# Attention, channel mix and mixer on one core: a pair's first two tiles of queries share one step for scores, one bias and one step for products

## The chip, the cores and the metric

The kernel runs on one core of a Trainium2 chip. Its engines are TensorE (PE, with PEld for the loading of weights), VectorE (DVE), ScalarE (ACT), GpSimd (POOL) and SyncE (SP), which issues the DMAs. Each engine works through its own instructions in order. The metric is the device time of one execution in microseconds, median of several runs.

## The reference

Three layers follow each other, all in fp32, for 4 batches of 576 tokens: attention with 8 heads of 64 and a mask by blocks of 64 tokens, a channel mix with a shift by one token, and a mixer over tokens and channels.

```python
def _attn_ref(q, k, v):                      # (4, 8, 576, 64) each
    scores = scale * np.matmul(q, k.transpose(0, 1, 3, 2))
    mask = block_i >= block_j                # blocks of 64 tokens
    scores = np.where(mask, scores, -1000000000.0)
    scores = scores - np.max(scores, axis=-1, keepdims=True)
    attn = np.exp(scores)
    attn = attn / (np.sum(attn, axis=-1, keepdims=True) + 1e-09)
    return np.matmul(attn, v).astype(np.float32)

def _moe_ref(x, mu_k, mu_r, w_k, w_v, w_r):  # x (4, 576, 512)
    xk = mu_k * x + (1.0 - mu_k) * x_prev    # x_prev: x one token earlier
    xr = mu_r * x + (1.0 - mu_r) * x_prev
    k = np.maximum(xk @ w_k, 0.0)
    v = k * k @ w_v
    r = 1.0 / (1.0 + np.exp(-(xr @ w_r)))
    return (r * v).astype(np.float32)

def _moe2_ref(x, w_tok1, w_tok2, w_ch1, w_ch2):
    h = np.maximum(x.transpose(0, 2, 1) @ w_tok1, 0.0) @ w_tok2
    u = x + h.transpose(0, 2, 1)
    h2 = np.maximum(u @ w_ch1, 0.0) @ w_ch2
    return (u + h2).astype(np.float32)
```

## The kernel before

**Layout.** The 8 heads are taken as 4 pairs. The 576 tokens of a batch are two parts: part 0 is tokens 0 to 255, with the query tiles j = 0 and 1 of 128 rows, part 1 is tokens 256 to 575, with j = 2, 3 and a last one, j = 4, of 64 rows for both heads together. `attention(b, hf)` issues, for each pair, the loads of q and k (`load_qk`) and of v (`load_v`, with v scaled to fp16 halves vb), one `unit` for each query tile, and `pv`.

**unit.** A tile's scores (L510) go into a PSUM tile s of two banks, one for each head; two such tiles are there. DVE masks the block above the diagonal (L538) and takes the negated maximum of the rows (L544), the bias is that times 0.125 (L553 on DVE; L551 on ACT for j = 1, by `nb_a`), ACT takes the exponentials with their sums (L563), and the reciprocal of the sum (L575 or L571, then L581) scales them. The probabilities become two fp16 tiles side by side in `pin`, a rounded one (`first`: L587 on ACT where j stands in `p1_act` or, in the batch's opening, `p1_first`, else DVE) and what the rounding left (`second`, L593 on DVE). A DMA from SP transposes pin into pt (`turn`, L599). `pv.products` multiplies pt with vb into the PSUM tile o (L646), `pv.total` scales o into xt (L655 on ACT for part 1, L657 on DVE for part 0).

**Channel mix.** For each part, `mix` builds the operands in fp32 pieces: mt (L720 ACT, L726 DVE), its high part xh (L732, on DVE for two of the four) and its low part xl (L736). `r_group` multiplies them with w_r (L751 for xh, L756 for xl) into a PSUM tile l, of which there are two, and `r_out` (L792, ACT) reads it; k_group, k_out and v_group follow in the same manner with w_k and w_v. The mixer's two stages, `front` and `back`, come behind all batches' attention; `back` fills the end of the span (L764).

**Weights.** `load_split` brings each weight in chunks through a DMA (L345), a cast on ACT (L352), a join on DVE (L355), a high part on ACT (L361) and a low part on POOL or DVE (L364). w_r and w_k come in chunks of 410 columns through a stage wst, w_v in 16 chunks of 256 columns through qkl and tw. These run beside the attention of batch 0.

**Order.** Nothing runs in the order in which it is written. Each piece of work is a `step` with an engine, an estimated cost, what it reads and writes, and a key. `Plan.schedule` plays all steps through a model and takes, on each engine, the ready step with the smallest key. The key is the step's due time less the numbers in PLAN: `lead_of` for its kind of step, `lead_begin` on top for the groups in `begin` (the weights of the first layers and batch 0), and `shift` for its group (a010 is attention of batch 0, part 1, pair 0; c00 the channel mix of batch 0, part 0).

Of the kernel before, what the change touches and what calls it, by code (L numbers as in the profile page):

```python
# [46 lines left out]
    nb_a=(1,), sm_a=(1,), ot_a=(1,), nq=(0, 1), sq_1=(), fifo=("xh", "xl", "l", "o", "xt0", "xt1", "qkh", "uh"),  # L47
    ft=3.02, fd=27.4576, cw=3.3876, tfr=24.8747, lx=0.15, lpe=0.2, lse=0.12, land=2.1,

    lead_of={  # L50
        "attention.edge": -710.03, "back.<lambda>": 34.98, "back.g_group": -21.39, "back.g_high": -674.45,
        "back.g_low": -16.35, "back.rest": 162.8, "back.split": -271.85, "back.store": -779.77, "back.y_group":
        -49.32, "back.y_out": 128.07, "channel_mix.k_group": 0.52, "channel_mix.k_high": 122.36, "channel_mix.k_low":
        49.5, "channel_mix.k_out": 700.87, "channel_mix.r_group": -1.88, "channel_mix.r_out": 38.93,
        "channel_mix.square": -490.37, "channel_mix.store": 972.64, "channel_mix.v_group": -4.31, "channel_mix.v_out":
        138.59, "front.back_in": 734.14, "front.h1_high": -268.59, "front.h1_low": -80.29, "front.hidden": 281.6,
        "front.high": 274.43, "front.load": 776.08, "front.low": 678.84, "front.sum_u": 443.53, "front.turn": -120.46,
        "load_qk.high": 253.03, "load_qk.load": 185.56, "load_qk.low": 404.0, "load_qk.whole": 421.84,
        "load_v.gather": -15.3, "load_v.largest": -10.87, "load_v.load": 459.86, "load_v.one": 31.7, "load_v.power":
        182.97, "load_v.scale": 265.33, "load_v.spread": 478.19, "load_v.two": 729.5, "mix.here": -3.03, "mix.high":  # L60
        -14.49, "mix.low": 3.37, "mix.shifted": 147.07, "pv.products": -2.92, "pv.total": 92.69, "split_chunk.high":
# [56 lines left out]
def c_v2(n):  # L118
    return 0.067 + n / 1920
# [186 lines left out]
class Kern:  # L306
# [1063 lines left out]
```

## Time and profile before

| | |
|---|---|
| time, median of 3 runs | 806.55 us (803.76 to 809.64) |
| profiled execution, its own time | 811.06 us |
| its span, first to last instruction | 809.3 us |
| mean granted clock of TensorE | 0.993 |
| busy: PE, DVE, ACT, POOL | 763.7, 477.3, 419.2, 181.3 us |
| matmuls | 6120 |

The profile is of one execution. The span lies 1.8 us under that execution's time, and the execution 4.5 us over the median. Times in views are microseconds from the start of the span unless marked ns; L12 is line 12 of the kernel. A group or row names output and inputs as out<-in; the granted clock is a share of full speed.

### The profile page before, as it was taken

What the parts mean: (1) busy time and instruction counts of PE and PEld (TensorE: products, weight loads), DVE (VectorE), ACT (ScalarE), POOL (GpSimd) and SP (SyncE); (2) the same over time, 40 slices, a digit from 0 to 9 for tenths busy, and PEclk for the clock granted to TensorE, in tenths of its full rate; (3) what the DMA queues carried; (4) which work ended last, traced back from release to release, by engine and by line L of the source; (5) the groups of instructions that cost most, each with busy time, mean ns of one, the idle gap of its engine ahead of it and who ended that gap; (6) DMA issues with size and microseconds to landing.
All of it is one profiled execution on the core that took longest, in us unless ns stands there. A gap on an engine that the chain in (4) does not pass through costs nothing.

```text
span 809.3 us, 16129 instructions
## 1 busy us (share of the span) xinstructions
PE 763.7 (94%) x6120; PEld 661.7 (82%) x6120; DVE 477.3 (59%) x1194; ACT 419.2 (52%) x1070; POOL 181.3 (22%) x209
## 2 busy tenths in 40 slices
PE   2459999998999999999999999999999999999998
PEld 1227899887989999999999989998888888888886
DVE  7897898997798987789555687612212302301210
ACT  6887978687678795778564565502201201301100
POOL 3433524334145142432443222200000000000000
PEclk9999999999899999999999999999999999999999
DMA  8976964686465843566552654200000010000001
GB/s 272 269 189 106 201 148 115 146 170 120 113 138 125 159 117 93 117 140 113 191 180 84 232 170 141 78 27 1 14 26 1 14 39 14 1 26 14 14 13 40
DMA packets 136750, 84.30 MB, mean 104 GB/s; under 512 B 110944, under 2 KB 118240, under 8 KB 136160
## 3 DMA queue, kind: packets, MB, share of 16 engines
q1 hardware_dynamic: 136672, 83.27, 41.8%
q8 instruction: 48, 0.79, 0.4%
q14 instruction: 30, 0.25, 0.1%
HBM read 47.58 MB, written 9.44 MB: 70 GB/s over the span
## 4 chain that ended last, share of the span: by engine, by line
PE 81%; DVE 7%; DMA 5%; ACT 5%; issue 2%; SPq 0%; POOL 0%; ACTq 0%; DVEq 0%
PE b L764 37%; PE l L751 18%; PE l L756 9%; PE s L510 5%; PE o L646 4%; PE b L938 3%; PE b L959 3%; DMA pt<-pin 3%; DVE pin L593 2%; DMA wst<-in_w_k 1%; PE b L914 1%; DVE nm L544 1%; ACT pin L587 1%; ACT p L563 1%; DMA qkl<-in_w_v 1%
## 5 line engine op out<-in xcount | busy, mean ns | idle before, releaser
L1030 ACT ACTIVATE wy<-b 128x512 fp32r<-128x512 f32 (+1 forms) x60 | 33.3, 555 | 211.8 <-PE b L764 211.2
L764 PE MATMUL b<-uh,wx 128*128 128x512 f32 (+1 forms) x480 | 139.6, 373 | 0.0
L751 PE MATMUL l<-xh,wx 128*128 128x256 f32 (+1 forms) x768 | 123.7, 302 | 2.2 <-ACT r L792 1.8
L751 PEld LDWEIGHTS l<-xh,wx 128*128 128x128 f32 x768 | 107.9, 190 | 7.4 <-ACT r L792 2.0
L764 PE MATMUL b<-wy,c2a 128*128 128x512 f32 (+1 forms) x460 | 110.8, 367 | 0.0
L764 PEld LDWEIGHTS b<-uh,wx 128*128 128x128 f32 x480 | 87.2, 188 | 17.3 <-issue 0.2
L764 PEld LDWEIGHTS b<-wy,c2a 128*128 128x128 f32 x460 | 79.2, 189 | 15.3
L593 DVE SCALAR_TENSOR_TENSOR pin<-p,rs,pin 128x128 f16<-128x128 f32 (+4 forms) x112 | 77.0, 707 | 7.5 <-ACT pin L587 7.3
L1045 DVE TENSOR_TENSOR x<-b,x 128x256 f32<-128x256 f32 (+7 forms) x32 | 13.5, 454 | 114.8 <-PE b L764 114.8
L751 PE MATMUL l<-kh,wy 128*128 128x256 f32 (+1 forms) x512 | 78.1, 304 | 0.2 <-DVE ve L428 0.2
L646 PEld LDWEIGHTS <-vb 128*64 128x64 f16 x1920 | 52.9, 115 | 29.8 <-issue 13.7
L646 PE MATMUL o<-pt,vb 128*64 128x128 f16 (+1 forms) x1920 | 62.4, 220 | 14.3 <-DMA pt<-pin 7.2
L764 PE MATMUL b<-gx,wx 128*128 128x512 f32 x192 | 75.4, 393 | 0.0
L751 PEld LDWEIGHTS l<-kh,wy 128*128 128x128 f32 x512 | 71.5, 194 | 2.5 <-issue 1.4
L563 ACT ACTIVATE p<-s,nb 128x384 f32<-128x384 f32 (+4 forms) x112 | 61.6, 553 | 19.2 <-DVE nb L553 9.7
L587 ACT ACTIVATE pin<-p,rs 128x128 f16<-128x128 f32 (+4 forms) x112 | 63.2, 588 | 13.2 <-DMA pt<-pin 6.9
L756 PE MATMUL l<-xl,wx 128*128 128x320 f32 (+1 forms) x384 | 68.2, 300 | 0.0
L544 DVE TENSOR_REDUCE nm<-s 128x2 f32<-128x256 f32 (+4 forms) x80 | 63.6, 798 | 1.9 <-PE s L510 1.3
L756 PEld LDWEIGHTS l<-xl,wx 128*128 128x128 f32 x384 | 56.6, 190 | 2.1 <-issue 1.2
L1033 DVE SCALAR_TENSOR_TENSOR wy<-b,wy 128x512 fp32r<-128x512 f32 (+1 forms) x28 | 16.1, 576 | 62.8 <-ACT wy L1030 62.7
L1033 DVE SCALAR_TENSOR_TENSOR gx<-b,wy 128x512 fp32r<-128x512 f32 x32 | 21.9, 690 | 47.8 <-ACT wy L1030 47.8
L736 POOL TENSOR_TENSOR xl<-mt,xh 128x256 fp32r<-128x256 f32 (+1 forms) x32 | 28.4, 891 | 91.7 <-DVE xh L732 52.5
(116 smaller groups left out, 1397.0 us busy)
## 6 DMA issues: line engine op xcount, KB each, us to landing
wst<-in_w_c SPq DMA_DIRECT2D x24, 256.0 KB, 2.7
qkf<-in_kq SPq DMA_DIRECT2D x12, 480.0 KB, 3.5
v<-in_v SPq DMA_DIRECT2D x16, 320.0 KB, 3.1
x<-xd SPq DMA_DIRECT2D x4, 1152.0 KB, 7.0
wst<-in_w_c2a SPq DMA_DIRECT2D x18, 256.0 KB, 2.7
qkl<-in_w_v SPq DMA_DIRECT2D x16, 256.0 KB, 3.4
wst<-in_w_k SPq DMA_DIRECT2D x9, 410.0 KB, 5.4
qkf<-in_kq SPq DMA_DIRECT2D x12, 256.0 KB, 2.9
```

The source lines that it names most:

```text
L510: self.nc.tensor.matmul(o, q[e, q0:q0 + P], k[e, k0:k1], start=n == 0, stop=n == len(terms) - 1)
L544: nc.vector.tensor_reduce(out=c["nm"][:, :nh], in_=m, axis=AX.XY if j == 4 else AX.X, op=ALU.max, negate=True)
L563: nc.scalar.activation(out=c[x], in_=s, func=AF.Exp, scale=0.125, bias=c["nb"][:, x:x + 1], accum_out=c["sm"][:, x:x + 1],)
L587: nc.scalar.activation(out=like(pin[:, :n]), in_=c[x], func=AF.Copy, scale=rs)
L593: nc.vector.scalar_tensor_tensor(out=like(pin[:, w:w + n]), in0=c[x], scalar=rs, in1=like(pin[:, :n]), op0=ALU.mult, op1=ALU.subtract)
L646: nc.tensor.matmul(o[hh * D:hh * D + D, q0:q0 + rows], v[:, i, y, hh, :], st["pt", hh, j][:, x * (j + 1) + i, :], start=i == x == y == 0, ...
L736: (nc.vector if i in pl["xl_d"] else nc.gpsimd).tensor_tensor(out=l, in0=x[i], in1=raw(x["h"][i]), op=ALU.subtract)
L751: self.nc.tensor.matmul(ps, ww[:, k, :], x[0][k], start=k == 0 and n == 0, stop=False)
L756: self.nc.tensor.matmul(ps, w[0][:, k, :], x[1][k], start=False, stop=k == kt - 1)
L764: self.nc.tensor.matmul(ps, ww[k], xx[k], start=k == 0 and n == 0, stop=k == kt - 1 and n == 2)
L1030: nc.scalar.activation(out=gh(m), in_=d["g", m][:, :n], func=AF.Relu)
L1033: nc.vector.scalar_tensor_tensor(out=gl(m), in0=d["g", m][:, :n], scalar=0.0, in1=raw(gh(m)), op0=ALU.max, op1=ALU.subtract)
```

## The change

`unit` takes a tuple of tiles. In part 0 a pair's tiles j = 0 and 1 are one unit: their scores are one step into one s tile, the second tile's columns behind the first's in each head's bank, and one bias instruction of 4 columns serves both (on DVE, as the unit's first tile, 0, isn't in `nb_a`). Maximum, exponentials, sums, roundings and transposes stay one for each tile and head. The products of tiles 0 and 1 are one step; those of 2, 3 and 4 stay single. Tile 2 leaves `p1_act`, so its `first` goes from ACT to DVE in batches 1 to 3 (24 instructions). `ft`, which sets when the mixer's first stage is due, goes from 3.02 to 2.94, and all of `lead_of`, `lead_begin` and `shift` have new numbers, so the whole program is ordered anew. The matmuls stay 6120, and the other totals of instructions stay but for the 16 biases and the 24 firsts.

```diff
-    wk=-29.6677, wv=-2.34, cpk=1.6637, cpv=2.1596, p1_act=(0, 1, 2, 3, 4), p1_first=(0, 1, 2, 3, 4), xl_d=(0, 2),
+    wk=-29.6677, wv=-2.34, cpk=1.6637, cpv=2.1596, p1_act=(0, 1, 3, 4), p1_first=(0, 1, 2, 3, 4), xl_d=(0, 2),
...
+    nb_a=(1,), sm_a=(1,), ot_a=(1,), nq=(0, 1), pj=((2,), (3,), (4,)), sq_1=(), fifo=("xh", "xl", "l", "o", "xt0",
+    "xt1", "qkh", "uh"), ft=2.94, fd=27.4576, cw=3.3876, tfr=24.8747, lx=0.15, lpe=0.2, lse=0.12, land=2.1,
...
-    def unit(self, key, st, heads, j, begin):
+    def unit(self, key, st, heads, js, begin):
...
+        nh = 1 if js == (4,) else 2
+        size = lambda j: P * (j + 1) if j < 4 else S
+
+        at, o = {}, 0
+        for j in js:
+            at[j] = o
+            o += size(j)
+        m = nh * len(js)
         c = {}
...
+        each = [(i, j, x) for i, j in enumerate(js) for x in range(nh)]
+        tp, tpin, tpt = ({(j, x): Buf(t or f"pt{j}") for _, j, x in each} for t in ("p", "pin", ""))
...
         def scores():
+            for j in js:
+                n, q0 = size(j), P * j - (j > 1) * NK0
+                if j < 4:
+                    self.qk(st, q0, [(s[:, y, at[j]:at[j] + n], half[y], 0, n) for y in range(2)])
+                else:
+                    self.qk(st, q0, [(s[:, y, :HT], slice(0, P), y * HT, (y + 1) * HT) for y in range(2)])
...
+        def bias():
+            c["nb"] = small("nb")
+            if first_j in pl["nb_a"]:
+                nc.scalar.mul(c["nb"][:, :m], c["nm"][:, :m], 0.125)
             else:
+                nc.vector.tensor_scalar(out=c["nb"][:, :m], in0=c["nm"][:, :m], scalar1=0.125, scalar2=None, op0=ALU.mult)
...
+        def first(i, j, x):
+            pin = c["pin", j, x] = self.pin[tpin[j, x].slot]
+            rs, out = c["rs"][:, row(i, x)], like(j, pin[:, :size(j)])
+            if act(j):
             else:
+                nc.vector.tensor_scalar(out=out, in0=c[j, x], scalar1=rs, scalar2=None, op0=ALU.mult)
...
+        step("PE", cost, key, scores, r=st["tqk"], w=[ts], mode="half" if nh == 2 else "")
+        for i, j in enumerate(js):
+            if j < 4:
+                step("V", 0.14, key, mask, j, w=[(ts, ("mask", j))])
+            n = size(j)
+            step("V", c_v(n if j == 4 else 2 * n), key, largest, i, j, r=[(ts, ("mask", j))], w=[(tnm, i)])
+        step(*(("A", 0.1) if first_j in pl["nb_a"] else ("V", 0.067)), key, bias, r=[tnm], w=[tnb], alone=nh == 1)
+        for i, j, x in each:
+            step("A", c_a(size(j), True, True) + 0.09, key + 0.3 * x, exps, i, j, x,
+                 r=[tnb] if here(j) else [ts, tnb], w=[(ts, (j, x)) if here(j) else tp[j, x], (tsm, (j, x))])
+        for i, j in enumerate(js):
+            r, w = [(tsm, (j, x)) for x in range(nh)], [(trs, j)]
+            step(*(("A", 0.1) if j in pl["sm_a"] else ("V", 0.067)), key, sums, i, j, r=r, w=w, alone=nh == 1)
+            step("V", 0.075, key, inverse, i, r=w, w=w)
+        for i, j, x in each:
+            n, k = size(j), key + 0.3 * x
+            p = (ts, (j, x)) if here(j) else tp[j, x]
+            pin = tpin[j, x]
+            on = ("A", c_a(n, here(j), True)) if act(j) else ("V", c_v(n, True) if here(j) else c_v2(n) + 0.06)
+            step(*on, k, first, i, j, x, r=[p, (trs, j)], w=[(pin, 0)], alone=here(j))
+            step("V", c_v(n, True), k, second, i, j, x, r=[p, (trs, j), (pin, 0)], w=[(pin, 1)], alone=here(j))
+            step("S", 1.24, k, turn, i, j, x, r=[pin], w=[tpt[j, x]], dma=0.224 * (j + 1))
...
-        def products(j):
+        def products(js):
+            for j in js:
+                products_of(j)
+
+        def products_of(j):
...
-        for j in PARTS[hf][2]:
-            step("PE", (0.06 if j < 4 else 0.04) * 4 * (j + 1) + 0.05, key, products, j,
-                 r=[st["tpt", 0, j], st["tpt", 1, j], vst["tvb"]], w=[(to, j)], mode="float16")
+        for js in ((0, 1),) if hf == 0 else PLAN["pj"]:
+            step("PE", sum((0.06 if j < 4 else 0.04) * 4 * (j + 1) for j in js) + 0.05, key, products, js,
+                 r=[st["tpt", x, j] for j in js for x in range(2)] + [vst["tvb"]], w=[(to, js)], mode="float16")
...
-                u = [0.0, 0.33]
-                for j in range(2):
-                    self.unit(t + dt * u[j], st, [0, 1], j, begin)
+                self.unit(t, st, [0, 1], (0, 1), begin)
             else:
                 u = [0.0, 0.32, 0.75]
                 for j in range(2, 5):
-                    self.unit(t + dt * u[j - 2], st, [0, 1], j, begin)
+                    self.unit(t + dt * u[j - 2], st, [0, 1], (j,), begin)
```

In the new kernel's line numbers, exponentials are L573, first L600 (ACT) and L602 (DVE), second L606, the bias on DVE L562, the mix L744, L750, L756 and L760, r_out L816.

The start of ACT's program; wst is the stage of w_r, p, sm and nb the exponentials, their sums and the bias of the first pair. Before:

```order
L563 ACT_TABLE_LOAD
L563 ACTIVATE p,sm<-s,nb 128x128
L352 CAST wst<-wst 128x410
L551 ACTIVATE nb<-nm 128x2
L563 ACTIVATE p,sm<-s,nb 128x128
L563 ACTIVATE p,sm<-s,nb 128x256
L361 CAST wx<-wst 128x410
L587 ACTIVATE pin_90<-p,rs 128x128
```

The table load stood with the exponentials of the first tile, and the bias of the second tile between them. The same engine and place, after:

```order
L352 ACT_TABLE_LOAD
L352 CAST wst<-wst 128x410
L573 ACTIVATE p,sm<-s,nb 128x128
L573 ACTIVATE p,sm<-s,nb 128x256
L361 CAST wx<-wst 128x410
L352 CAST wst<-wst 128x410
L573 ACTIVATE p,sm<-s,nb 128x128
L352 CAST wst<-wst 128x410 x2
```

The table load now stands with the cast of w_r's first chunk, which has moved ahead of all exponentials; those of tile 0 and tile 1 follow each other without a bias between.

ACT around the first r_out (r<-l) of batch 0, part 0; qkl and tw are a chunk of w_v, mt and xh the operands of the mix, xt the output of attention. Before:

```order
L732 CAST xh<-mt 128x256
L720 ACTIVATE mt<-xt_133,omu 128x256
L352 CAST tw_64<-qkl 128x256
L361 CAST wy<-qkl 128x256
L655 ACTIVATE xt_593<-o,vo 128x320
L720 ACTIVATE mt<-xt_131,omu 128x256
L792 ACTIVATE r<-l 128x256
L563 ACTIVATE p,sm<-s,nb 128x384
L361 CAST wy<-qkl 128x256
L732 CAST xh<-mt 128x256
```

The first r_out stands four rows behind a cast of w_v (L352). The same place on ACT, after:

```order
L352 CAST tw_63<-qkl 128x256
L744 ACTIVATE mt<-xt_137,omu 128x256
L361 CAST wy<-qkl 128x256
L744 ACTIVATE mt<-xt_133,omu 128x256
L573 ACTIVATE p,sm<-s,nb 128x384
L756 CAST xh<-mt 128x256
L816 ACTIVATE r<-l 128x256
L352 CAST tw_64<-qkl 128x256
L756 CAST xh<-mt 128x256
L681 ACTIVATE xt_569<-o,vo 128x320
L361 CAST wy<-qkl 128x256
```

It now stands six rows behind one such cast and just ahead of the next, and part 1's total (xt, L655 before, L681 after) has moved from ahead of it to behind it.

DVE in batch 1, at a first tile 2 of part 1 (p and pin of 384 columns, after) and at the same stretch of rows before; kh and kl are operands of the channel mix. Before:

```order
L593 SCALAR_TENSOR_TENSOR pin_90<-p,rs,pin_90 128x128
L538 MEMSET s 64x2x64
L544 TENSOR_REDUCE nm<-s 128x2
L593 SCALAR_TENSOR_TENSOR pin_91<-p,rs,pin_91 128x128
L593 SCALAR_TENSOR_TENSOR pin_93<-s,rs,pin_93 128x256
L553 TENSOR_SCALAR nb<-nm 128x2
L845 CAST kh<-kt 128x320
L848 TENSOR_TENSOR kl<-kt,kh 128x320
L593 SCALAR_TENSOR_TENSOR pin_92<-s,rs,pin_92 128x256
```

Here each second (L593) has its first on ACT. DVE in the same stretch of its program, after:

```order
L562 TENSOR_SCALAR nb<-nm 128x4
L562 TENSOR_SCALAR nb<-nm 128x2
L750 SCALAR_TENSOR_TENSOR mt<-xt_1116,mu,mt 128x256
L602 TENSOR_SCALAR pin_90<-p,rs 128x384
L756 CAST xh<-mt 128x256
L606 SCALAR_TENSOR_TENSOR pin_90<-p,rs,pin_90 128x384
L602 TENSOR_SCALAR pin_91<-p,rs 128x384
L587 TENSOR_SCALAR rs<-sm 128x2
L594 RECIPROCAL rs<-rs 128x2
L606 SCALAR_TENSOR_TENSOR pin_91<-p,rs,pin_91 128x384
```

Two firsts (L602, 128x384) have come into DVE's row, each ahead of its second (L606), and the bias of a pair's two tiles is one instruction of four columns.

## Rows read from the trace of the kernel before

**Rows 1.** Page, parts 1 and 4: busy us, share and instructions; the last chain's shares

```profile
PE 763.7 (94%) x6120; PEld 661.7 (82%) x6120; DVE 477.3 (59%) x1194; ACT 419.2 (52%) x1070; POOL 181.3 (22%) x209
...
PE 81%; DVE 7%; DMA 5%; ACT 5%; issue 2%; SPq 0%; POOL 0%; ACTq 0%; DVEq 0%
```

**Rows 2.** Windows: length, busy us of each engine, granted clock, DMA share, GB/s

```profile
0.00:62.00 62.00, 27.86 (x160) 13.69 (x162) 53.51 (x150) 48.11 (x130) 25.77 (x34) 1.00 0.88 243
...
69.90:74.00 4.10, 4.10 (x20) 3.90 (x20) 3.32 (x10) 4.10 (x14) 1.47 (x2) 0.58 0.44 132
74.00:197.00 123.00, 122.21 (x1421) 109.16 (x1420) 108.02 (x296) 102.63 (x274) 46.41 (x51) 1.00 0.68 143
197.00:208.00 11.00, 7.95 (x88) 7.34 (x88) 5.65 (x16) 5.64 (x18) 3.88 (x5) 0.69 0.93 165
208.00:400.00 192.00, 189.89 (x2209) 175.57 (x2208) 161.26 (x422) 146.71 (x383) 65.30 (x69) 1.00 0.56 124
400.00:511.00 111.00, 111.00 (x733) 102.65 (x732) 75.31 (x167) 62.67 (x150) 33.66 (x43) 1.00 0.52 169
```

**Rows 3.** Timeline of PE: start, us, what [idle before, releaser]

```profile
69.90 1.56 PE L751 MATMUL l<-xh,wx 128*128 128x256 f32 x8 [1.76 <-ACT r L792]
...
201.91 1.86 PE L646 MATMUL o<-pt,vb 128*64 128x128 f16 x31 [2.82 <-DMA pt<-pin]
```

**Rows 4.** Timelines of ACT, SP and DVE around 62 to 70 us

```profile
68.00 0.48 ACT L352 CAST tw<-qkl 128x256 f16<-128x256 bf16 x1 [3.62 <-DMA qkl<-in_w_v]
69.48 0.37 ACT L792 ACTIVATE r<-l 128x256 f32<-128x256 f32 x1
...
62.01 0.86 SPq L345 DMA_DIRECT2D qkl<-in_w_v  x1
...
63.93 0.27 DVE L732 CAST xh<-mt 128x256 fp32r<-128x256 f32 x1
```

**Rows 5.** Chain of waits in order of time: start, us, what

```profile
69.90 1.56 PE l L751 x8
...
78.69 0.95 PE l L751 x8
...
86.91 1.01 PE o L646 x32
...
112.99 1.92 PE l L751 x16
...
203.77 3.60 PE l L751 x16
```

**Rows 6.** ACT's first instructions; tile wst: DMAs, durations, time to landing

```profile
6.55 1.28 ACT L563 ACT_TABLE_LOAD   x1 [6.55 <-DVE nb L553]
7.85 0.37 ACT L563 ACTIVATE p<-s,nb 128x128 f32<-128x128 f32 x1
8.21 0.64 ACT L352 CAST wst<-wst 128x410 f16<-128x410 bf16 x1
...
L345 SPq DMA_DIRECT2D wst<-in_w_r x4: 432/432/432, 2.6 to 4.0; - x4
...
DMA to landing us min/median/max: 5.5/6.3/7.2
```

**Rows 7.** Groups by line and form: xcount | busy us, mean ns | idle before, releaser

```profile
L593 DVE SCALAR_TENSOR_TENSOR pin<-p,rs,pin 128x384 f16<-128x384 f32 x32 | 21.6, 690 | 1.8 <-ACT pin L587 1.6
...
L587 ACT ACTIVATE pin<-p,rs 128x384 f16<-128x384 f32 x32 | 19.0, 612 | 2.3 <-DMA pt<-pin 1.8 <-DVE xt L681 0.4
...
L446 DVE SCALAR_TENSOR_TENSOR vb<-v,vs,vb 128x640 f16<-128x640 f32 x16 | 18.2, 1138 | 1.8 <-ACT vb L443 1.7
...
L544 DVE TENSOR_REDUCE nm<-s 128x2 f32<-128x768 f32 x16 | 15.1, 946 | 0.1
...
L593 DVE SCALAR_TENSOR_TENSOR pin<-s,rs,pin 128x256 f16<-128x256 f32 x24 | 11.0, 479 | 6.4 <-ACT pin L587 6.1
...
L544 DVE TENSOR_REDUCE nm<-s 128x2 f32<-128x512 f32 x16 | 10.8, 678 | 0.1
...
L355 DVE SCALAR_TENSOR_TENSOR qkl<-qkl,tw 128x256 uint32<-128x256 uint32 x16 | 8.1, 505 | 2.7 <-ACT tw L352 2.7
...
L732 DVE CAST xh<-mt 128x320 fp32r<-128x320 f32 x16 | 5.3, 337 | 0.0
...
L551 ACT ACTIVATE nb<-nm 128x2 f32<-128x2 f32 x16 | 3.2, 201 | 1.1 <-DVE nm L544 0.9
```

More of the change, by code (lines that the diff above doesn't have):

```diff
@@ L48 @@
-    ft=3.02, fd=27.4576, cw=3.3876, tfr=24.8747, lx=0.15, lpe=0.2, lse=0.12, land=2.1,
+    nb_a=(1,), sm_a=(1,), ot_a=(1,), nq=(0, 1), pj=((2,), (3,), (4,)), sq_1=(), fifo=("xh", "xl", "l", "o", "xt0",
+    "xt1", "qkh", "uh"), ft=2.94, fd=27.4576, cw=3.3876, tfr=24.8747, lx=0.15, lpe=0.2, lse=0.12, land=2.1,
     lead_of={
[L51 to L61, printed above, removed]
-        -63.89, "split_chunk.join": 6.76, "split_chunk.load": 143.85, "split_chunk.low": 282.21, "split_chunk.top":
-        -112.45, "unit.bias": 105.96, "unit.exps": -239.76, "unit.first": -135.83, "unit.inverse": 471.77,
-        "unit.largest": 1.71, "unit.mask": -0.69, "unit.scores": 481.59, "unit.second": 298.83, "unit.sums": 7.56,
-        "unit.turn": -61.72,
@@ new lines @@
+        185.59, "front.back_in": 1124.06, "front.h1_high": -95.34, "front.h1_low": -7.08, "front.hidden": 575.4,
+        "front.high": 539.5, "front.load": 951.26, "front.low": 879.84, "front.sum_u": 705.05, "front.turn": -293.4,
+        "load_qk.high": 205.12, "load_qk.load": 584.15, "load_qk.low": 147.07, "load_qk.whole": 506.8,
+        "load_v.gather": -17.03, "load_v.largest": -21.68, "load_v.load": 418.12, "load_v.one": 230.69,
+        "load_v.power": 513.99, "load_v.scale": 250.78, "load_v.spread": 450.42, "load_v.two": 681.14, "mix.here":
@@ new lines @@
+        -4.95, "mix.high": 30.93, "mix.low": 17.72, "mix.shifted": 349.13, "pv.products": 11.11, "pv.total": 128.96,
+        "split_chunk.high": -127.18, "split_chunk.join": 12.93, "split_chunk.load": 510.1, "split_chunk.low": 672.28,
+        "split_chunk.top": -253.27, "unit.bias": 235.66, "unit.exps": -360.91, "unit.first": -227.18, "unit.inverse":
+        277.04, "unit.largest": -13.48, "unit.mask": 47.55, "unit.scores": 841.0, "unit.second": 253.51, "unit.sums":
+        112.87, "unit.turn": 392.45,
@@ L91 @@
-        19.35, "mix.low": 63.96, "mix.shifted": 223.54, "pv.products": -1.86, "pv.total": 4.3, "split_chunk.high":
-        191.37, "split_chunk.join": -2.04, "split_chunk.load": -58.89, "split_chunk.low": -104.87, "split_chunk.top":
-        225.28, "unit.bias": 146.72, "unit.exps": 56.02, "unit.first": 220.91, "unit.inverse": -61.06, "unit.largest":
-        0.1, "unit.mask": 86.57, "unit.scores": 187.42, "unit.second": -42.99, "unit.sums": -11.55, "unit.turn":
-        -135.86,
+        "attention.edge": 193.5, "back.<lambda>": 170.91, "back.g_group": 188.34, "back.g_high": -146.25,
@@ new lines @@
+        "front.high": 482.71, "front.load": -138.31, "front.low": -393.74, "front.sum_u": 336.72, "front.turn": 55.86,
+        "load_qk.high": -498.1, "load_qk.load": -466.89, "load_qk.low": 760.96, "load_qk.whole": 7.71,
+        "load_v.gather": 317.87, "load_v.largest": -38.89, "load_v.load": -52.74, "load_v.one": 414.52,
+        "load_v.power": 31.61, "load_v.scale": 52.73, "load_v.spread": -277.94, "load_v.two": -477.87, "mix.here":
+        -8.16, "mix.high": 98.86, "mix.low": 144.06, "mix.shifted": 68.56, "pv.products": 100.12, "pv.total": -28.59,
@@ L96 @@
+        "split_chunk.high": 314.93, "split_chunk.join": 159.29, "split_chunk.load": -39.85, "split_chunk.low":
+        -187.23, "split_chunk.top": 211.97, "unit.bias": 74.62, "unit.exps": -178.98, "unit.first": 254.2,
+        "unit.inverse": 89.37, "unit.largest": 40.19, "unit.mask": 30.33, "unit.scores": 49.76, "unit.second": -38.72,
+        "unit.sums": 8.33, "unit.turn": -463.54,
     },
```

135 lines of the change are left out of this document (55 added, 80 removed), and 16 rows, old and new, of the table shift.

## The prediction

> **What bounds the kernel now.** The page's busy shares come first: TensorE (PE) is busy for 94% of the span, VectorE (DVE) for 59%, ScalarE (ACT) for 52%, and the chain that ended last is 81% PE [rows 1]. So PE's work is the floor, and this change leaves PE's work alone: the same 6120 matmuls, in another order. What it can win or lose is idle time of PE and time at half clock. The table of windows says where these lie [rows 2]. In the first 62 us PE has 27.86 us of work, so 34 us pass without it; DVE is busy for 53.51 of them and the DMA engines for 0.88 of their time. From 74 to 197 us PE works 122.21 of 123, from 208 to 400 us 189.89 of 192, from 400 to 511 us 111.00 of 111, and the tail behind 511 us is the last mixer alone, which the change doesn't order anew in any way that shows. Two short places remain. At 69.90 PE had waited 1.76 us for ScalarE's r [rows 3], and in the 4.10 us behind that the granted clock is 0.58 [rows 2]. At 201.91 it had waited 2.82 us for a transposed probability tile [rows 3], and the window around it has 7.95 us of PE in 11 at a clock of 0.69 [rows 2].
>
> The price of each is read from the chain [rows 5]. Eight matmuls of 256 columns take 0.95 us on their normal step and 1.56 at 69.90; sixteen of 320 take 1.92 and, at 203.77, 3.60. [...] First place: 1.76 + 4.10 x (1 - 0.58) = 3.5 us. Second place: 11 - 7.95 = 3.05 idle, 3.60 - 1.92 = 1.7 on the sixteen, and about 0.85 on the 31 products that took 1.86 [rows 3] against 32 in 1.01 [rows 5]: 5.6 us.
>
> **The change part by part.** The sum is made against the profiled execution, 811.06 us (span 809.3); the median shown is 806.55, that is 4.5 lower, and the difference is carried over unchanged.
>
> Merged steps, 0. The scores and the products of a pair's first two tiles have the same matmuls as before, and in the order before, the products of both tiles already stand without a gap in 12 of 16 pairs. Over the whole kernel PE changes kind of work 213 times where it was 218. Nothing there is worth a microsecond. That the first tile's exponentials now wait for the second tile's scores and maximum costs one 128x512 maximum, 0.678 us [rows 7], of lead; from 65 us on PE waits 0.79 us in 123 [rows 2], so the lead hides it. If that cover went, 16 x 0.678 = 10.8 us is the far end, which I don't take.
>
> One bias, 0. Sixteen biases of 0.201 us leave ACT [rows 7], and DVE's stays, with four columns in place of two. ACT is busy for 102.63 of 123 us in the long stretch [rows 2] and doesn't gate it.
>
> The opening, +0.8. Three rows speak. (a) ACT's first instruction was the table load for the exponentials, at 6.55, with the first exponential at 7.85 [rows 6]. In the new order a cast of w_r comes first (first order fence). Its DMA is issued at 2.60 and takes 5.5 us at least [rows 6], so it lands at 8.1, and if the table load stands behind the same wait ACT starts 1.55 us late; if not, the cast's 0.64 us alone is put ahead. Between 0 and +1.55 I take the upper end, +1.5, since the exponentials of the first pair feed DVE, which bounds these 62 us. (b) DVE has up to the last high part of the first r operands (63.93 in the trace [rows 4]) four more joins of w_v at 0.505 us [rows 7], +2.0, but two seconds of 384 columns less (0.690 each) and one maximum of 768 columns, -2.3, and small ones, -0.4: -0.7 net. (c) Four more chunks of w_v (256 KB) are loaded by then: 1.05 MB at the opening's 243 GB/s [rows 2] is 4.3 us, if the queue were the bound; at a DMA share of 0.88 it is near it, so I keep +4.3 as an upper end and take 0, as DVE ends last there.
>
> First place at 69.90, -3.5. ACT stood for 3.62 us until 68.00 in the cast of a w_v chunk, whose DMA was issued at 62.01, and r_out came behind it at 69.48 [rows 3, 4]. In the new order the first r_out has a chunk's cast six rows ahead and the next one behind it (second fence), and by PE's rows in the new order 72 products and a scores step stand among the r groups, which covers a late r. So the wait should go, and the half clock with it. What is late next is DVE's mix there, whose work to the same point is shorter by (b). Ends: 0 to -3.5.
>
> The first roundings on DVE, +2.7. 24 instructions (tile 2 of batches 1 to 3) leave ACT, 0.612 us each [rows 7], and become DVE instructions. No row has this form; the nearest is DVE's cast of 128x320, 0.337 us [rows 7], so I take 24 x 0.337 = 8.1 us on DVE, 8 of them (2.7 us) in batch 1. To the end of batch 1 the new order has DVE do more at the same place of PE's program: these 2.7, three maxima of 0.678, one vb of 1.138, two seconds of 0.479 [rows 7], in all 6.8 us. DVE is busy 108.02 of 123 us there [rows 2], 15 us free. The maxima, the vb and the seconds are later work drawn ahead and are paid back; the firsts are not. Between 0 (all in idle time) and +6.8 (nothing hidden) I take the firsts alone, +2.7, near the middle since the busy share of 0.88 already leaves little room for an engine that works in order.
>
> [...]
>
> Second place at 201.91, 0: its wait is for the chain first, second, transpose, and the new order has as many such chains in each batch as the old; that one of them comes late is as likely as before. Ends: -5.6 to +5.6 (a second one like it).
>
> Sum: 0 + 0 + 0.8 - 3.5 + 2.7 + 0 = 0.0. That is 811.06 for the profiled execution, and **806.5** for the median.
>
> **Rivals.** (A) Faster: both places go. For it: ACT loses 14.7 us of firsts and 3.2 of biases, and the chain to the transposes loses an ACT-DVE handover in tile 2; against it: the same chain needs more DVE, the busier of the two in the stretch [rows 2]. Price: 0.8 - 3.5 - 5.6 = -8.3, 798.2 us. Chance 0.22. (B) Slower: DVE becomes the bound between 74 and 400 us. Mechanism: a first behind a maximum or a mix on DVE holds its second, its transpose and so the products, and PE stands still and falls to half clock. It decides once DVE's share there goes over some 0.93 (108.02 + 6.8 of 123). For it: the 0.88 now. Against it: DVE sits idle for 15 us. Price: +6.8 and one more spell like that at 201.91, +5.6, with the opening's 0.8 and the first place gone, -3.5: +9.7, 816.2 us. Chance 0.24. (C) The change doesn't do what it says: the merging is no merging, as 12 of 16 pairs were already together, and only the reshuffled order acts, with the opening's queue as its price: +4.3 in place of (c)'s 0, 810.8 us, within 1% and so inside the forecast's class.
>
> **How the numbers follow.** About 1% (8 us, so 798.5 and 814.6) is what a measurement of this kernel can tell from no change. The forecast with C has 0.54, from 802 to 812 (the ends of the first place and of DVE's term). A has 0.22, B 0.24. A lies at 798.2 and B at 816.2; the range takes in both centres and about half of what lies beyond: 797 to 818. Faster by over 1%: 0.22; within: 0.54; slower: 0.24.
>
> **What would show it.** PE without a wait for r near 70 us and no clock of one half there: the first place was right. ACT's first exponential at 9 to 10 us: (a). DVE busy above 0.9 between 74 and 197 us with PE still at 122 of 123: the firsts are hidden, and the time falls below the forecast by up to 2.7. PE waiting there for transposes, with DVE never idle before them: B. A count of waits on transposes of two or more like the one at 201.91 would make me wrong to the slow side, none of them to the fast side; an opening that ends much before or after 65 us would make me wrong in either, since 34 us of PE's idle time lie in it and I move them by 0.8 only.

## The result, and the profile after

| | before | after |
|---|---|---|
| time, median | 806.97 us, 8 runs (803.76 to 810.4) | 812.38 us, 8 runs (811.21 to 813.70) |
| profiled execution, span | 811.06, 809.3 us | 812.32, 810.5 us |

The ratio is 1.0065, 95% interval 1.0041 to 1.0088: 5.4 us slower, where no change was forecast. A second set of runs of the same kernel, below, gave 1.0106 (1.0074 to 1.0137). The loss is 5 to 8 us.

The page of the changed kernel, parts 1 and 4, as [rows 1]:

```profile
PE 755.8 (93%) x6120; PEld 657.4 (81%) x6120; DVE 487.0 (60%) x1218; ACT 410.1 (51%) x1030; POOL 187.1 (23%) x209
...
PE 79%; ACT 7%; DVE 5%; DMA 4%; issue 3%; POOL 1%; SPq 1%; ACTq 0%; POOLq 0%; DVEq 0%
```

DVE has gained 9.7 us and ACT lost 9.1, and the matmuls are the same. PE's share of the last chain has fallen from 81 to 79%. So PE waits more or is later, and the windows say where. Those of the changed kernel, columns as in [rows 2]:

```profile
0.00:62.00 62.00, 19.32 (x144) 11.23 (x144) 50.62 (x139) 46.03 (x123) 28.86 (x37) 0.62 0.86 242
...
74.00:197.00 123.00, 119.52 (x1419) 105.89 (x1419) 111.06 (x312) 97.54 (x259) 45.34 (x46) 1.00 0.70 145
197.00:208.00 11.00, 11.00 (x135) 9.89 (x134) 10.46 (x28) 8.13 (x22) 3.49 (x5) 1.00 0.76 132
208.00:400.00 192.00, 187.75 (x2168) 174.33 (x2167) 159.25 (x418) 138.64 (x357) 66.56 (x68) 0.99 0.57 119
240.00:260.00 20.00, 20.00 (x143) 17.95 (x143) 14.63 (x41) 11.08 (x26) 7.83 (x9) 0.92 0.31 73
400.00:511.00 111.00, 110.88 (x746) 103.48 (x745) 76.75 (x169) 63.90 (x156) 35.19 (x44) 1.00 0.55 174
```

Four things differ from [rows 2]. In the first 62 us PE was busy for 19.32 us in place of 27.86, at a granted clock of 0.62. From 74 to 197 us it was busy for 119.52 in place of 122.21. The place at 197 to 208 us, 7.95 us of work at 0.69 before, is now full at 1.00. PE worked 2.1 us less between 208 and 400, about a new place: the window from 240 to 260 has a clock of 0.92. PE's timeline of the changed kernel shows what stood ahead of that:

```profile
238.94 1.76 PE L775 MATMUL l<-xh,wx 128*128 128x320 f32 x8 [2.03 <-DVE ve L428]
```

PE waited 2.03 us for a small maximum of v's scale (ve, L428 on DVE), and the eight matmuls behind it took 1.76 us. In the second trace of this kernel, below, the same eight take 1.44 at a clock of 1.00; here the clock fell to 0.50 from 240.50 to 243.30 us. There is no wait for r near 70 us, as forecast. But that wait turned out to be a chance of the one profiled execution, as the first experiment shows.

ACT's start in the changed kernel, timeline, as [rows 6]:

```profile
8.22 1.28 ACT L352 ACT_TABLE_LOAD   x1 [8.22 <-DMA wst<-in_w_r]
9.52 0.65 ACT L352 CAST wst<-wst 128x410 f16<-128x410 bf16 x1
10.04 0.36 ACT L573 ACTIVATE p<-s,nb 128x128 f32<-128x128 f32 x1
```

The table load stands behind the DMA of w_r, 1.67 us later than before, and the first exponential is at 10.04 in place of 7.85. The four totals of batch 0's part 0 (xt<-o,vo on DVE), which close one pair each, show what the opening became. Each row has the count, the durations, and the start of the first and of the last. The kernel before:

```profile
L657 DVE TENSOR_SCALAR xt<-o,vo x4: 470/471/479, 27.9 to 59.1; 128x256 f32<-128x256 f32 x4
```

The kernel after:

```profile
L683 DVE TENSOR_SCALAR xt<-o,vo x4: 466/473/479, 31.2 to 63.2; 128x256 f32<-128x256 f32 x4
```

Each pair is 3 to 5 us late: 27.9, 36.3, 47.7, 59.1 became 31.2, 41.7, 51.5, 63.2.

### The profile page after: what moved, and what is told of

The parts are those of the page before. It is cut to its first block, busy times and chain, and to the rows that moved or that the text cites. A ratio compares the mean times of both kernels' runs of the same rounds, so it can differ in the third digit from the quotient of the medians.

```text
span 810.5 us, 16056 instructions
## 1 busy us (share of the span) xinstructions
PE 755.8 (93%) x6120; PEld 657.4 (81%) x6120; DVE 487.0 (60%) x1218; ACT 410.1 (51%) x1030; POOL 187.1 (23%) x209
## 4 chain that ended last, share of the span: by engine, by line
PE 79%; ACT 7%; DVE 5%; DMA 4%; issue 3%; POOL 1%; SPq 1%; ACTq 0%; POOLq 0%; DVEq 0%
PE b L788 37%; PE l L775 17%; PE l L780 9%; PE s L510 4%; PE o L672 4%; PE b L962 3%; PE b L983 3%; ACT pin L600 2%; DVE pin L606 1%; DMA pt<-pin 1%; DMA qkl<-in_w_v 1%; PE b L938 1%; ACT p L573 1%; ACT qkh L491 1%; ACT s L573 1%
## 5 line engine op out<-in xcount | busy, mean ns | idle before, releaser
L672 PE MATMUL o<-pt,vb 128*64 128x128 f16 (+1 forms) x1920 | 60.5, 218 | 20.1 <-DMA pt<-pin 11.8
L606 DVE SCALAR_TENSOR_TENSOR pin<-p,rs,pin 128x128 f16<-128x128 f32 (+4 forms) x112 | 73.3, 668 | 8.0 <-ACT pin L600 7.4
L573 ACT ACTIVATE p<-s,nb 128x128 f32<-128x128 f32 (+3 forms) x112 | 62.0, 555 | 19.1 <-DVE nb L562 9.9
L780 PE MATMUL l<-xl,wx 128*128 128x320 f32 (+1 forms) x384 | 68.3, 300 | 0.0
L553 DVE TENSOR_REDUCE nm<-s 128x2 f32<-128x256 f32 (+4 forms) x80 | 62.5, 797 | 1.0 <-PE s L510 0.6
L600 ACT ACTIVATE pin<-p,rs 128x128 f16<-128x128 f32 (+4 forms) x88 | 49.4, 584 | 8.7 <-DVE rs L594 4.7
L760 POOL TENSOR_TENSOR xl<-mt,xh 128x256 fp32r<-128x256 f32 (+1 forms) x32 | 30.8, 964 | 90.8 <-DVE xh L756 74.6
L872 POOL TENSOR_TENSOR kl<-kt,kh 128x256 fp32r<-128x256 f32 (+1 forms) x40 | 35.6, 894 | 47.1 <-ACT kh L869 29.6
```

What stands on the lines that cost most here:

```text
L553: nc.vector.tensor_reduce(out=c["nm"][:, nh * i:nh * i + nh], in_=s, axis=AX.XY if j == 4 else AX.X, op=ALU.max, negate=True)
L573: nc.scalar.activation(out=c[j, x], in_=s, func=AF.Exp, scale=0.125, bias=c["nb"][:, row(i, x)], accum_out=c["sm"][:, row(i, x)],)
L600: nc.scalar.activation(out=out, in_=c[j, x], func=AF.Copy, scale=rs)
L606: nc.vector.scalar_tensor_tensor(out=like(j, pin[:, w:w + n]), in0=c[j, x], scalar=rs, in1=like(j, pin[:, :n]), op0=ALU.mult, op1=ALU.subt ...
L672: nc.tensor.matmul(o[hh * D:hh * D + D, q0:q0 + rows], v[:, i, y, hh, :], st["pt", hh, j][:, x * (j + 1) + i, :], start=i == x == y == 0, ...
L760: (nc.vector if i in pl["xl_d"] else nc.gpsimd).tensor_tensor(out=l, in0=x[i], in1=raw(x["h"][i]), op=ALU.subtract)
```

## The experiments

Two rulers are used beside the time. The totals of the four pairs say how late the opening is. They scatter: four traces with the changed kernel's opening (two of the kernel itself, two of experiments that leave the opening alone, firsts_on_act and ve_first) have the first total at 30.5 to 31.5 us and the fourth at 62.6 to 63.8, so a shift of 1 us in one trace shows little. The loss of PE says where in the program a kernel falls behind another of a different order: each matmul is given the usual interval between two of its form (all kernels have 705 us of such work), and the time less the work done by then is what PE has lost. Only differences between kernels count there, and they are good to about half a microsecond. Kernels with one and the same order of PE are matched matmul by matmul instead.

**The kernel before, again.** The same code, profiled a second time. 

> The kernel before, unchanged, for a second trace and for the spread. Measured against itself: ratio 1.000. The profiled execution of before (811.06 us) lay 4.1 us over its median of 806.97 and held a wait of 2.82 us for a transpose at 201.91 with half clock behind it, 5.6 us in all. If that stall is in a part of the executions only, this trace lacks it whenever its execution lies near 806, and the trace of the changed kernel has to be compared with a base without it. If the stall is in every execution, it is there again at 200 to 208 us and the 4.1 us lie elsewhere.

 It took 806.76 us (ratio 0.9999, 0.9975 to 1.0023). The windows of its trace:

```profile
30.00:62.00 32.00, 18.49 (x106) 8.49 (x108) 29.87 (x81) 27.16 (x73) 12.68 (x13) 1.00 0.88 232
69.90:74.00 4.10, 4.10 (x30) 3.25 (x29) 3.94 (x12) 3.96 (x12) 2.38 (x4) 1.00 0.26 70
74.00:197.00 123.00, 120.31 (x1426) 107.34 (x1425) 109.34 (x292) 102.00 (x274) 45.94 (x51) 1.00 0.74 148
197.00:208.00 11.00, 9.56 (x123) 8.83 (x123) 6.71 (x23) 5.85 (x19) 1.43 (x2) 0.84 0.57 130
```

Behind 69.90 the clock is 1.00, not 0.58 [rows 2], and PE waited for nothing there. Matched matmul by matmul, the first trace is 0.5 us later at 65 us, 4.0 later at 70 and 3.9 later at 120: the whole stall is that one execution's. This trace has 808.25 us, near the median, and no trace of the experiments below that keep this order up to there, or nearly (merge_later, firsts_on_dve, hold_products, four_less_before), has that wait: the median doesn't hold the 3.5 us. The second place stands in both: 2.82 us of wait in the first trace, 2.77 in this one.

**The changed kernel, again.** 

> The changed kernel, unchanged, as a second trace and as the measure for the three runs beside it: 811 to 814 us. Its first profiled execution had PE at half clock from 10 to 65 us, and its other executions show a mean clock of 0.991 to 0.999 at the same times. If the half clock of the opening costs nothing, this trace has the same times behind 70 us with or without it.

 It took 814.34 us (1.0106, 1.0074 to 1.0137; profiled 812.42). Its trace agrees with the first: totals from 30.7 to 63.0, the wait of 2.06 us for ve at 239.96. It is the base for what follows.

**Code and numbers apart.** The new code with the old numbers, and the old code with the new ones. The engine of tile 2's firsts goes with the numbers.

```diff
# merge_old_numbers, against the changed kernel: PLAN of before, with
+    pj=((2,), (3,), (4,)),
# old_code_new_numbers, against before: the whole PLAN of the changed kernel
```

> The changed code (merged scores, one bias, merged products) with the numbers of the kernel before, p_1 of tile 2 on ScalarE. Theory opening (the merged step itself costs, as the first exponential waits for both tiles' maxima and a two-bank score tile is held for four exponentials): +2 to +4 us against before, 809 to 811, with the first exponential near 9 us. Theory DVE or theory order: within 1 us of before, 806 to 808, apart from what chance re-ordering does, which may be some us either way.

> The code before (single steps for each tile, two biases) with all numbers of the changed kernel, the firsts of tile 2 on VectorE among them. Theory order (the new numbers put work in a worse row): slower by 4 to 6 us, 811 to 813, as the changed kernel. Theory opening (merged step): 807 to 809. Theory DVE: 810 to 813, as the firsts are on VectorE here too; the run with the firsts on ScalarE then tells it from theory order.

They took 822.32 us (1.0174, 1.015 to 1.0197) and 835.62 us (1.0349, 1.0311 to 1.0387). Merging alone costs some 14 us, the numbers alone 28, both together 5 to 8: neither half can be priced by itself. The merged code has a late opening under the old numbers too (totals from 31.8 to 62.9). The old code starts its exponentials as early as ever under the new ones (7.8), and its fourth total comes at 72.8.

**The firsts.** Tile 2's roundings back on ACT in the changed kernel, and on DVE in the kernel before, each in its frozen order (the plan is not told).

```diff
# firsts_on_act
-            if act(j):
+            if act(j) or j == 2:
# firsts_on_dve
-            if p1_act:
+            if p1_act and (begin or j != 2):
```

> The changed kernel in exactly its order, but the 24 firsts of tile 2 are issued to ScalarE at the places where they stood, as in the kernel before. Theory DVE: the firsts took 0.598 us each on VectorE (14.1 us) and make it late, seen in PE's waits for the reading of the l tile on VectorE (1.22 and 2.03 us); then this gives back 3 to 5 us of the 5.4 lost: 807.5 to 809.5 us. Theory opening: nothing of it, 811.5 to 813. Theory order: also 811 to 813, or a loss, since ScalarE then has work that its order was not made for.

> The kernel before in exactly its order, with the 24 firsts of tile 2 in batches 1 to 3 issued to VectorE at the places where ScalarE had them. In the changed kernel's order, putting them back on ScalarE cost some 2 to 3 us. Theory (the move pays in itself, since it takes a handover and 14.7 us off ScalarE): 1 to 2.5 us faster than before, 804 to 805.5, which would beat both kernels. Theory DVE of the prediction (the move costs 2.7 us): 808 to 810. Rival (an order made for one engine is upset by the other, whichever way): slower by 2 to 4 us, 808 to 810.5, as it was the other way round.

On ACT: 815.73 us (1.0091, 1.0063 to 1.0118), which the time can't tell from the changed kernel; matmul by matmul its one trace is 1.0 us behind the changed kernel's second trace by 242 us and 2.1 by 400. On DVE: 811.7 us (1.0077, 1.0047 to 1.0107), slower than before. So the move loses in the old order, and taking it back wins nothing in the new one: DVE's extra work is not what makes the changed kernel slow.

**The opening's first instructions, and the wait for ve.** The changed kernel's order, frozen, with the first pair's exponentials, v scale, roundings and transposes ahead of w_r's casts and joins; then with three of the scale's maxima (L428, with what follows from them) moved ahead on DVE; then both.

```diff
# open_fixed
+        behind(top, exps[2])
+        behind(join, largest[0])
...
# ve_first
+        for a, o in (("a202", find("unit.inverse", "a203")[1]), ("a101", find("unit.inverse", "a101")[1]),
+                     ("a301", [s for s in find("channel_mix.k_high", "c21") if s.eng == "V"][2])):
+            behind(find("load_v.scale", a)[0], o)
```

> The changed kernel in exactly its order but for the first 15 us: the first pair's exponentials stand ahead of the first cast of w_r on ScalarE, its v scale, roundings and transposes ahead of the joins of w_r's other chunks, as before. Theory opening (ScalarE's start at 9.5 us, v's scaling at 14.2 where it was 11.5, is what puts all four totals of the first part 3.4 to 5.4 us later): those totals come 2 to 3 us earlier and the time falls by 2 to 3 us, 809 to 810.5. Rival (the opening is held by VectorE's and the DMA queue's whole work up to 63 us, four more joins and loads of w_v among it, so an early start is lost again): totals within 1 us of now from the second pair on, time 811.5 to 813.

> The changed kernel in exactly its order but for three instructions: VectorE reads the largest of v (the l tile) of three pairs ahead of the roundings that stood before it. In the trace those roundings stretched to 2.29 us beside GpSimd, and PE waited 1.22, 2.03 and 0.38 us for the l tile, with half clock behind the second. Theory (these waits are a third of the loss against the kernel before): the three waits go and the time falls by 3 to 4.5 us, 808 to 809.5. Rival (the waits are covered, or PE waits for the next thing in their place): within 1 us of now, 811.5 to 813.

> Both of these edits together. If both theories hold the gains add, 5 to 7.5 us, and the time is 805 to 807.5, that is the time of the kernel before or less. If only the waits for the l tile count: 808 to 809.5. If neither counts: 811 to 813.

Against 1.0106 of the changed kernel, measured together with them: 812.12 us (1.0082, 1.0057 to 1.0108), 812.64 (1.008, 1.0055 to 1.0105) and 812.40 (1.0077, 1.0055 to 1.01). The intervals overlap, so the traces decide. In the first, the first exponential stands at 8.99, the totals at 29.6 to 61.9, and PE is 1.1 us ahead of the changed kernel's second trace at 60 us and at the end. But both together have the same opening, with that exponential at 9.11, and their totals stand at 31.0 to 63.1, no earlier than in the changed kernel: that an early start of ACT carries through is not shown. The second takes most of its wait away, as PE's timeline of that kernel shows:

```profile
239.65 1.44 PE L811 MATMUL l<-xh,wx 128*128 128x320 f32 x8 [0.39 <-DVE ve L464]
```

It is 1.7 us faster from 200 to 240 us, where it had been 1.4 behind the changed kernel's trace, and 0.9 behind it at 400: what the wait gave back went elsewhere. Both together are 0.8 ahead at the end, which they gain at this wait.

**Less of w_v.** Chunks 2 to 5 of w_v are neither loaded nor cast, in either kernel; GpSimd writes zeros in their place.

```diff
+        gone = tok[0] == "wv" and 2 <= tok[1] < 6
```

> The changed kernel in its order, with chunks 2 to 5 of w_v's 16 left out (their load, cast, join, high and low parts; zeros stand in their place), so that by 63 us as many chunks have been brought in as in the kernel before. The opening is 4 to 5 us later than before by 86 us, and an earlier start of ScalarE gave back 1.1 of it. Theory opening by its whole work: 2 us of joins on VectorE and 1.05 MB on the queue go, the four totals of the first part come 2 to 4 us earlier, and the time falls by 2 to 4 us against the changed kernel (812.4): 808.5 to 810.5. Rival (the chains of each pair, not the amount of work, hold the opening): totals within 1 us, time 811.5 to 813.

> The same four chunks left out of the kernel before, as the control. If the price of a chunk in the opening is a general one, it gains as much as the changed kernel does, 2 to 4 us (802.5 to 804.5). If the queue there has room, it gains less than 1 us (805.5 to 807).

811.86 us (1.0076, 1.0048 to 1.0104) and 804.92 us (0.9987, 0.9965 to 1.0009). Without a megabyte of loads the changed kernel's totals come at 30.6 to 62.5, half a microsecond early, and its PE is 1.1 us ahead at 65 us; in the kernel before, the fourth total comes 1.6 us early. Both are far from the 4.3 us that a bound queue would give back. The queue is not what holds the opening.

**Merging a part.** The old numbers, with tiles merged in batch 0 alone, or in batches 1 to 3 alone; then in batch 0 with a bias for each tile; then only batch 0's products merged.

```diff
# merge_first, merge_later (not begin)
+                if begin:
+                    self.unit(t, st, [0, 1], (0, 1), begin)
# first_two_biases, on top of merge_first
+        if len(js) == 2:
+            for i, j in enumerate(js):
+                step(*(("A", 0.1) if j in pl["nb_a"] else ("V", 0.067)), key, bias, i, r=[(tnm, i)], w=[(tnb, i)])
# products_first
+                for j in range(2):
+                    self.unit(t + dt * u[j], st, [0, 1], (j,), begin)
...
+        for js in (((0, 1),) if merged else ((0,), (1,))) if hf == 0 else PLAN["pj"]:
```

> The numbers of the kernel before, tile 2's firsts on ScalarE, and the merged step in batch 0 alone. Theory opening by the merged step (the first exponential waits for both tiles' maxima, and each pair's work goes through in one lump): the four totals stand at about 31, 42, 52 and 63 us, as in both merged kernels so far, where before has 27.8, 36.3, 47.6 and 59.0; PE is 4 us behind by 86 us; the time is 810 to 812. Rival (the new numbers' order did it): totals within 1 us of before, 806 to 808.

> The numbers of the kernel before, tile 2's firsts on ScalarE, and the merged step in batches 1 to 3 alone; up to 95 us the order is that of the kernel before. With merging in all batches these numbers gave 822, 16 us over before. Theory opening: 4 of the 16 lie in batch 0, so this one has 816 to 820, most of which would be the old numbers not fitting the new steps. Rival (merging in the full stretch is free, and only batch 0 pays): 806 to 809.

> The code of before with the old numbers, tiles 0 and 1 merged in batch 0's part 0 alone (one score step, one s tile, one step of products), but with a bias for each tile, so that the exponentials of tile 0 don't wait for the maximum of tile 1. If the wait for both maxima is what delays the opening, the totals of part 0's four pairs come back to near 28, 36, 48 and 59 us and the time to near 806 to 808. If it is the rest (both tiles' scores in one step and one s tile, so that only two units of two tiles fit in PSUM's score tiles), they stay near 32, 43, 54 and 63 us, and the time near 816 to 820.

> The code of before with the old numbers, and in batch 0's part 0 the products of tiles 0 and 1 as one step; scores, s tiles and biases stay single. If merged products cost nothing (the prediction's 0), the totals stay near 28, 36, 48 and 59 us and the time within 806 to 809. If the products' merging holds the pairs up, the totals move by 2 us or more and the time goes over 812.

| kernel | time, us | ratio (interval) | totals of the four pairs |
|---|---|---|---|
| merge_first | 819.15 | 1.0154 (1.0129 to 1.0179) | 32.7, 43.5, 54.3, 63.7 |
| merge_later | 812.82 | 1.0077 (1.006 to 1.0094) | 27.7, 35.6, 47.9, 59.4 |
| first_two_biases | 818.76 | 1.0146 (1.0104 to 1.0187) | 31.6, 42.4, 53.2, 62.6 |
| products_first | 825.79 | 1.0212 (1.0155 to 1.0268) | 28.3, 39.7, 55.4, 68.3 |

Merging in batch 0 makes the opening late; merging elsewhere leaves its order, and its times, as they were. A bias for each tile stands 1.1 us ahead of merge_first, but only 0.2 to 0.3 ahead of merge_old_numbers (31.8, 42.8, 53.5, 62.9), whose order up to 62 us is that of merge_first on every engine. In all three ACT's table load waits for w_r's first chunk and starts at 8.79 (merge_first), 8.51 (merge_old_numbers) and 7.35 us, so the 1.1 us are no more than that landing. The wait for both maxima is not shown to cost anything in the opening. The last row was the surprise: one step for the products alone, with nothing else merged, makes the fourth total 9 us late.

**Joined products in the old order.** That can be the joining or the order that the plan makes of it. So the order of before was frozen, and in all 16 pairs tile 0's products put directly ahead of tile 1's.

```diff
+        for g in (f"a{b}0{p}" for b in range(4) for p in range(NP)):
...
+                r.remove(one)
+                r.insert(r.index(two), one)
```

> The code of before with its order kept on every engine, but for one thing: in all sixteen pairs the products of tile 0 stand directly ahead of those of tile 1 on PE, as one merged step would (in 12 of 16 they already do). If merged products cost nothing by themselves, this gives 806 to 808 us and totals at 28, 36, 48 and 59 us, and the 826 us of the kernel that merges the products in batch 0 alone are the doing of the order that the plan makes of it. If the wait for both tiles' transposes is the price, the totals of batch 0 come 2 us or more later and the time is over 811.

807.48 us (1.0024, 1.0005 to 1.0043). Its totals, in the same view as above:

```profile
L707 DVE TENSOR_SCALAR xt<-o,vo x4: 472/474/477, 27.9 to 59.4; 128x256 f32<-128x256 f32 x4
```

And those of products_first:

```profile
L683 DVE TENSOR_SCALAR xt<-o,vo x4: 466/472/477, 28.3 to 68.3; 128x256 f32<-128x256 f32 x4
```

Joined in all pairs, products cost 1.4 us by themselves (0.4 to 3.5 by the interval). The rest of products_first's 19 us comes from the order. That much is shown; why the order is so bad is read from the code alone: the plan takes a step only when all that it reads is there, so a step of two tiles turns up later in its model, and other work goes first.

## Why the prediction was wrong

What PE has lost by a time, in us, puts the places in a row:

| by | before, again | after | after, again | merge_first | merge_later |
|---|---|---|---|---|---|
| 86 us | 58.1 | 62.8 | 62.8 | 64.2 | 58.4 |
| 195 us | 70.8 | 77.7 | 78.0 | 82.3 | 75.6 |
| 220 us | 77.7 | 80.0 | 80.8 | 85.8 | 80.9 |
| 260 us | 82.6 | 86.5 | 86.0 | 91.9 | 85.9 |
| 520 us | 97.1 | 101.3 | 101.3 | 108.1 | 101.5 |

From the first column to the second: opening +4.7, to 195 us +2.2, second place -4.6, to 260 us +1.6, the rest +0.3, in all +4.2. The trace of before in that column lies 1.5 us over its own median (808.25 against 806.76) and that of after at its median, which makes 5.7 where 5.4 was measured.

**First place, -3.5, and the difference of 4.5 carried over.** This is the step that failed. The wait went, as forecast, but the median had never had it. The profiled execution lay 4.5 us over the median, and the stall of 3.5 to 4 us in it was most of that difference. The prediction took the stall off as a gain and took the same 4.5 us off again as the way to the median. Without that credit its own terms give 810.0. That the miss is no larger is luck: the second place, which the sum held at 0, gave 4.6 us back.

**The opening, +0.8.** Wrong in size, and the second step that failed: it is some +4.7 by 86 us. Part (a) came as forecast and a little later, the first exponential at 10.04 for 9 to 10: the table load waits for the chunk (1.67 us later) and the cast stands ahead of the exponential as well, where the prediction took one or the other. Its worth is open, 1.1 us in open_fixed and none in open_and_ve. Part (c)'s upper end has the right size and the wrong cause, since four_less gives back 0.5. What was missed is that merging, with the order that the plan makes of it, delays the opening by itself: merge_first is late under the old numbers too, +6.1 by 86 us. In the window from 30 to 62 us the kernel before (again) did 18.49 us of PE's work, at full clock, and the changed kernel's second trace this:

```profile
30.00:62.00 32.00, 11.72 (x88) 6.62 (x88) 28.46 (x79) 27.43 (x73) 14.56 (x16) 1.00 0.87 223
```

DVE is as busy in both (28.46 and 29.87 of 32), and PE is busy for 6.8 us less; behind 62 us it has little room left (busy for 26.60 of 28 us from there to 90). PE's timeline of that trace shows it at the last pair:

```profile
59.60 0.32 PE L672 MATMUL o<-pt,vb 128*64 128x128 f16 x2 [3.53 <-ACT vb L443]
60.52 1.39 PE L672 MATMUL o<-pt,vb 128*64 128x128 f16 x22 [0.60 <-DVE vb L446]
61.84 3.36 PE L510 MATMUL s<-qk 64*128 64x384 f32 x8
```

And in the second trace of the kernel before:

```profile
54.91 0.32 PE L646 MATMUL o<-pt,vb 128*64 128x128 f16 x2 [0.17 <-ACT vb L443]
```

The last pair's vb is 4.7 us later, PE stands 3.53 us at it in its order, and part 1's scores stand behind.

**Merged steps, 0.** Nearly right for the products' instructions (hold_products, +1.4 us) and wrong for the program: the merged step is also another object for the plan. That the lead of 0.678 us is hidden "from 65 us on" was a reason about the wrong stretch, since merging shows before 65 us. merge_later shows that batches 1 to 3 weren't free under the old numbers either (4.5 us between 86 and 195 us in the table); the new ones bring that stretch to 2.2.

**One bias, 0.** Nothing speaks against it: first_two_biases has its totals 0.2 to 0.3 us ahead of merge_old_numbers, less than traces of one order differ.

**The firsts, +2.7.** Mis-sized, and not a loss. The group of the changed kernel:

```profile
L602 DVE TENSOR_SCALAR pin<-p,rs 128x384 f16<-128x384 f32 x24 | 14.1, 598 | 0.4 <-DMA pt<-pin 0.3
```

It is 14.1 us where 8.1 was taken, 598 ns each where the row of the cast has 337. DVE is 0.90 busy from 74 to 197 us, the sign named for hidden firsts, though PE is at 119.52 and not at 122: before_again has 120.31 there, so the 122.21 of [rows 2] belongs to the execution with the stall just ahead of it. The 2.2 us that the changed kernel loses from 86 to 195 us have another source. PE's waits for DVE there, 2.65 us in all, lie between 104 and 125 us, and the first of the firsts starts at 139.3. The longest, in PE's timeline:

```profile
120.80 1.44 PE L775 MATMUL l<-xh,wx 128*128 128x320 f32 x8 [1.22 <-DVE ve L428]
```

From 150 to 195 us, where most of batch 1's firsts stand, the two kernels lose the same, 4.9 and 5.0 us by the same ruler, and firsts_on_act, without the firsts on DVE, has those waits too.

**Second place, 0.** It went: a gain of 4.6 us, inside the ends of 5.6. Another of its kind came at 239 us, with ve in the transposes' part, 2.03 and 2.06 us of wait in the two traces. So 0 was some 3 us off. Nor does the place's going need the change: with the old order nearly kept, PE waits 0.75 us there in hold_products and not at all in four_less_before. The sixteen matmuls by which the prediction prices the place have 256 columns, not 320; the price of 1.7 us stays.

**The rivals.** B names DVE as the bound. Waits of PE for DVE did come, but none of those above stands behind a first, and firsts_on_act speaks against the firsts as their cause. A's gain at the second place came and was paid away in the opening. C gave 810.8 with the opening's price, nearest to the truth, but for the queue, which four_less rules out.

**What stays open.** Changed one at a time, the bias, ACT's start, w_v and joined products move the opening by at most 1.1, 1.1, 1.1 and 0.5 us (by the totals or PE's matmuls), none clearly beyond the scatter of traces of one order. The rest wasn't split by an experiment between the shared tile of scores and the order that the plan makes. PE's rows speak against late scores. These are the last ones of part 0 in batch 0, on PE's timeline in the first trace of the kernel before and then of the changed kernel:

```profile
31.69 1.23 PE L510 MATMUL s<-qk 64*128 64x256 f32 x4 [0.58 <-ACT p L563]
```

```profile
23.57 1.65 PE L510 MATMUL s<-qk 64*128 64x128 f32 x8 [5.43 <-ACT p L573]
```

The changed kernel has these scores earlier and the totals later, so the time is lost between them, where ACT and DVE work in a new order. The kernel before couldn't be put in a merged order by moving rows alone: with one tile of scores for each query tile, a pair takes both, and the next scores wait for exponentials that wait in turn. No kernel here that does the whole work beats the one before.

## What to carry to other kernels

A stall that is seen in one trace is a gain only if the median has it: profile the base a second time before taking credit for it, above all where that execution lies over the median. Where a planner orders the work, a merged step is not priced by its instructions; freeze the old order and make the edit inside it, and the two parts of the price come apart. And compare traces of one and the same order first: here their openings differ by up to 1.4 us, and a gain of that size in one trace is not yet one.

## What the runs showed of the hardware

**The firsts that overlapped GpSimd's TENSOR_TENSOR took up to 2.09 us.** Of the 24 firsts in the first trace of the changed kernel 17 took 0.34 to 0.42 us, and seven took 0.77 to 2.09. All seven overlap a TENSOR_TENSOR of GpSimd and end 0.21 or 0.22 us behind its end; none of the 17 started with more than 0.1 us of one still to run. DVE's timeline in the changed kernel:

```profile
292.17 2.78 DVE L602 TENSOR_SCALAR pin<-p,rs 128x384 f16<-128x384 f32 x2 [0.34 <-DMA pt<-pin]
```

GpSimd's at the same time:

```profile
291.81 2.24 POOL L495 TENSOR_TENSOR qkl<-qkf,qkh 128x960 fp32r<-128x960 f32 x1 [3.87 <-ACT qkh L491]
```

The first of the two starts 0.36 us behind GpSimd's start and takes 2.09. The wait of 2.03 us for ve has such an overlap ahead of it. DVE:

```profile
236.39 2.29 DVE L606 SCALAR_TENSOR_TENSOR pin<-p,rs,pin 128x128 f16<-128x128 f32 x1
238.60 0.28 DVE L428 TENSOR_REDUCE ve<-l 128x1 f32<-128x128 f32 x1
```

GpSimd:

```profile
236.31 2.22 POOL L495 TENSOR_TENSOR qkl<-qkf,qkh 128x960 fp32r<-128x960 f32 x1
```

A second of 128 columns, 0.34 us for the next one at 239.25, took 2.29 and ended 0.15 us behind GpSimd's end, and PE stood behind the maximum that came next. The second trace has the same pair: 2.29 us at 237.41 on DVE, beside 2.23 us at 237.33 on GpSimd. What holds DVE up there was not shown. That the old order loses when the firsts move to DVE (firsts_on_dve, 1.0077) is in line with these rows, but wasn't tried by moving GpSimd's work.

**The opening at a clock of 0.62 was 0.2 to 0.5 us later than at 1.00.** The first trace of the changed kernel has a clock of 0.62 in the first 62 us, of which PE was busy for 19.32, the second 1.00. Their totals differ by 0.2 to 0.5 us (63.2 and 63.0 for the last), and at 90 us PE's matmuls are 0.2 apart.
